# Fused chunk-sparse attention and ELU MLP on one core: a list scheduler with optional TensorE fillers, a lane model for DMAs, and another set of order parameters

## The chip, the core and the metric

The kernel runs on one core of one Trainium2 chip. The metric is device time in microseconds (us), lower is better. The kernel before takes 299.21 us, the median of three runs (298.0 to 299.57). TensorE is called PE here, its weight loads PEld, VectorE DVE, ScalarE ACT, GpSimd POOL and SyncE SP.

## The reference

Attention over 4 batches, 8 heads, 768 positions and 64 dimensions, in which each query keeps only 6 of 24 chunks of 32 keys, followed by an MLP with the ELU function. Cut to what matters:

```python
k_min = np.min(k_chunks, axis=3); k_max = np.max(k_chunks, axis=3)       # per chunk of 32 keys
ub = np.sum(np.maximum(q * k_min, q * k_max), axis=-1)                  # bound per query and chunk
ub = np.where(causal, ub, -1e9)
top_chunks = np.argsort(ub, axis=-1)[..., -6:]
scores = np.where(selected & causal_by_position, scale * q @ k.T, -1e9)
attn = softmax(scores)
x = (attn @ v) rearranged to [3072, 512]
h = x @ w_in                                                             # 512 -> 2048
out = where(h > 0, h, exp(min(h, 0)) - 1) @ w_out                        # 2048 -> 512
```

## The kernel before, in words

**Tiling.** The work is cut into eight parts i = 0 to 7: batch b = i // 2 and half h = i % 2 of the 768 positions, 384 queries each. Heads go in four pairs r = 0 to 3. For each part there are four kinds of work:

- `load` and `prep` (lines 415 to 515), once per pair: six DMAs of 96 KB bring K, Q and V of two heads (`kf`, `qf`, `vf`; line 412 issues them). TensorE transposes K and Q against an identity (L455), ACT or DVE copies them out of PSUM (L461, L463), DVE reduces K to chunk minima and maxima (L475), POOL or DVE places copies in `lhs` and `rhs` (L465), and POOL casts V to bf16 (L512). The casts are collected in the list `casts` in the order of the parts and pairs.
- `select` (lines 517 to 573), once per part, for all four pairs: TensorE forms the bounds (L529), DVE transposes them (L542), finds the sixth largest with MAX8 (L551), compares (L557), transposes back (L563) and writes the mask rows into `rhs` (L571).
- `attend` (lines 579 to 682), once per pair: scores (L595), exp on ACT into `pt` (L607, L613), the causal triangle on DVE (L622, L631), P·V (L651), the division on DVE (`rcp` L662, `on` L665), a transpose on TensorE (L676) and a copy to `xt` (L681). A pair of the second half uses five `pt` tiles, one of the first half two.
- `mlp` (lines 684 to 734), once per part: 16 groups of four matmuls with w_in (L693), for each of them exp on ACT (`e` L701), minus one on POOL (`m` L705) and ELU on DVE (`gT` L709); then three output tiles of 16 matmuls with w_out (L720) over all 16 `gT`, a copy (L728, L730) and a store.

The weights come in four pieces each, by casting DMAs on POOL's queue (`load_w_in` L365, `load_w_out` L372). Piece n waits for the V cast whose count stands in `T["gate"]`: the first four entries are for w_in, the last four for w_out, and an entry of 9 means the ninth cast.

**Fillers.** Lines 744 to 754 make operations called "fill": two matmuls of zeros, 512 columns wide, into a free PSUM bank (L750), with the lowest priority. Each one depends on the one before the last.

**What sets the order.** Nothing is emitted as it is written. `Graph.op` records each operation with its possible engines, costs, buffers, dependences and a priority, and `Graph.run` (lines 109 to 245) goes through time, event by event, and gives each idle engine the operation of lowest priority number that is ready and for which its buffers are free. The order in which operations start in this plan is the order in which they are emitted, on all engines, and each engine's instructions run in that order on the chip. `T` (lines 41 to 44) holds the number of buffers of each kind (`kf`, `pt`, `gT` and others) and the priorities: `attw` and `mlp` place the attention parts and the MLP parts, `prepa` and `loada` bring preparation and loads forward, `vlate` sets V loads and casts back, `sela` moves `select`, `evo`, `mf` and `sf` shift single steps, `gate` is for the weights, `fill` is the number of fillers.

In the plan, a DMA issued by SP or ACT may start while fewer than eight such transfers are under way (`flying[1] < 8`); which eight does not matter, and the count falls when the bytes are moved. The plan ends when every operation has been placed, the fillers too (`left`).

Of the kernel before, what the change touches and what calls it, by code (L numbers as in the profile page):

```python
# [36 lines left out]
PE, ACT, DVE, POOL, SP = "PE", "ACT", "DVE", "POOL", "SP"  # L37
SEM = 45.0


T = dict(kst=8, ubT=1, pstep=0.1397, kf=4, qf=4, vf=8, pt=9, xt=6, gT=18, qt=5, qr=4, rhs=5,
         nfirst=4, vlate=6.3955, gate=[2, 2, 6, 7, 7, 8, 9, 10], attw=[9.917, 18.912],
         mlp=[13.416, 15.5], loada=0.7909, prepa=10.9783, sela=-2.0944, fill=40, cold=6,
         evo=0.1849, mf=0.2655, sf=0.7044)


class Buf:
# [19 lines left out]
class Graph:  # L67
# [41 lines left out]
    def run(self, at=None, dma_lat=(700.0, 900.0)):  # L109
        free = {n: [(0.0, s) for s in range(len(v))] for n, v in self.slots.items()}  # L110
        engines = (PE, ACT, DVE, POOL, SP)
        at = {e: (at or {}).get(e, 0.0) for e in engines}
        avail = {e: [] for e in engines}
        events = sorted({0.0, *at.values()})
        arriving = []
        rings = {e: [] for e in (SP, ACT, POOL)}
        share = {SP: 1.0, ACT: 1.0, POOL: 7.0}
        flying = [0, 0]
        dma_at, asked = 0.0, -1.0
        port_free = {DVE: 0.0, POOL: 0.0}  # L120
        for o in self.ops:
            o.wait = len(o.deps)
            o.ready = 0.0
            if o.wait == 0:
                heapq.heappush(arriving, (0.0, o.seq, o))
        left = len(self.ops)
        order = []

        def settle(o):
            for b in o.bufs:  # L130
                b.left -= 1
                b.end = max(b.end, o.finish + SEM)
                if b.cls == "bank":
                    b.used[o.engine] = o.finish + SEM
                    heapq.heappush(events, o.finish + SEM)
                if b.left == 0 and b.cls in free:
                    free[b.cls].append((b.end, b.slot))
                    heapq.heappush(events, b.end)
            for n in o.nexts:
                n.wait -= 1  # L140
                n.ready = max(n.ready, o.finish + SEM)
                if n.wait == 0:
                    heapq.heappush(arriving, (n.ready, n.seq, n))
                    heapq.heappush(events, n.ready)

        def transfer(t):
            nonlocal dma_at, asked
            if asked <= t:
                asked = -1.0
            while True:  # L150
                live = [(r, share[e]) for e, r in rings.items() if r and r[0][0] <= dma_at]
                total = sum(w for _, w in live)
                later = [r[0][0] for r in rings.values() if r and r[0][0] > dma_at]
                stop = min([t] + later)
                if live:
                    stop = min(stop, dma_at + min(r[0][1] / w for r, w in live) * total)
                    for r, w in live:
                        r[0][1] -= (stop - dma_at) * w / total
                dma_at = stop
                for r, _ in live:  # L160
                    if r[0][1] <= 1e-6:
                        o = r.pop(0)[2]
                        flying[o.engine != POOL] -= 1
                        o.finish = dma_at + dma_lat[1]
                        settle(o)
                if dma_at >= t:
                    break
            live = [r for r in rings.values() if r]
            if live:
                due = max(t, min(r[0][0] for r in live)) + min(r[0][1] for r in live) + 1.0  # L170
                if not due - 40.0 < asked <= due + 40.0:
                    asked = due
                    heapq.heappush(events, due)

        while left or any(rings.values()):
            if not events:
                held = {n: len(v) for n, v in free.items()}
                stuck = [o.name for e in engines for _, _, o in avail[e]][:40]
                raise RuntimeError(f"stuck: {left} left, free {held}, {stuck}")
            t = heapq.heappop(events)  # L180
            while events and events[0] <= t:
                heapq.heappop(events)
            transfer(t)
            while arriving and arriving[0][0] <= t:
                _, _, o = heapq.heappop(arriving)
                for e in o.engines:
                    bisect.insort(avail[e], (o.prio, o.seq, o))
            moved = True
            while moved:
                moved = False  # L190
                for e in engines:
                    if at[e] > t:
                        continue
                    lst = avail[e]
                    pick = None
                    i = 0
                    while i < len(lst):
                        o = lst[i][2]
                        if o.start is not None:
                            lst.pop(i)  # L200
                            continue
                        ok = o.xfer is None or e == POOL or flying[1] < 8
                        need = {}
                        for b in o.bufs if ok else ():
                            if b.slot is None:
                                need[b.cls] = need.get(b.cls, 0) + 1
                                if sum(ft <= t for ft, _ in free[b.cls]) < need[b.cls]:
                                    ok = False
                                    break
                            elif b.cls == "bank" and any(x != e and ft > t for x, ft in b.used.items()):  # L210
                                ok = False
                                break
                        if ok:
                            pick = o
                            lst.pop(i)
                            break
                        i += 1
                    if pick is None:
                        continue
                    o = pick  # L220
                    dur, lat = o.engines[e]
                    o.engine, o.start = e, t
                    if e == POOL or (e == DVE and o.port):
                        held = max(0.0, port_free[DVE if e == POOL else POOL] - t)
                        dur, lat = dur + held, lat + held
                        port_free[e] = t + dur
                    at[e] = t + dur
                    heapq.heappush(events, at[e])
                    for b in o.bufs:
                        if b.slot is None:  # L230
                            fl = free[b.cls]
                            k = min((ft, s, j) for j, (ft, s) in enumerate(fl) if ft <= t)[2]
                            b.slot = fl.pop(k)[1]
                    if o.xfer is None:
                        o.finish = t + lat
                        settle(o)
                    else:
                        flying[e != POOL] += 1
                        rings[e].append([t + dur + dma_lat[0], o.xfer, o])
                        heapq.heappush(events, t + dur + dma_lat[0] + o.xfer)  # L240
                    order.append(o)
                    left -= 1
                    moved = True
        self.span = max(o.finish for o in order)
        return order
# [28 lines left out]
def kernel(  # L274
# [16 lines left out]
    def slots(cls, n, shape, dtype, pool=const):  # L291
        store[cls] = [pool.tile(shape, dtype, name=f"{cls}{i}") for i in range(n)]
        g.cls(cls, range(n))
# [4 lines left out]
    slots("bank", 8, [P, 512], F32, psum)  # L298
    slots("kf", T["kf"], [P, 3, 2, D], F32)
    slots("qf", T["qf"], [P, 3, 2, D], F32)  # L300
    slots("vf", T["vf"], [P, 3, 2, D], F32)
    slots("kt", 3, [P, HS], BF16)
    slots("lhs", 8, [P, 2, S], BF16)
    slots("vext", 8, [P, 6, 2, D + 1], BF16)
    for h in range(2):
        slots(f"rhs{h}", T["rhs"], [P, 2, HS], BF16)
    slots("kst", T["kst"], [P, 2, CHUNK], F32)
    slots("qt", T["qt"], [P, HS], F32)
    slots("qr", T["qr"], [P, HS], F32)
# [488 lines left out]
```

## Time and profile before

| | |
|---|---|
| median of 3 runs | 299.21 us (298.0 to 299.57) |
| the profiled execution's own time | 297.61 us |
| its span, first to last instruction | 295.8 us |
| mean granted clock of TensorE | 0.988 |
| PE busy (matmuls) | 282.7 us, 96% of the span |
| PEld busy (weight loads) | 173.0 us, 58% |
| DVE busy | 223.3 us, 75% |
| ACT busy | 202.0 us, 68% |
| POOL busy | 134.8 us, 46% |
| filler matmuls (L750) | 21.5 us of PE in 76 recorded matmuls |
| SP and ACT loads, POOL weight loads | 24.39 + 0.79 MB and 4.19 MB |

The span is also cut into 40 equal slices of 7.4 us, with the busy tenths of each engine, the clock that TensorE was granted and the share of the 16 DMA engines. A share over 1 means that packets overlapped on an engine. The busy time of a matmul reaches beyond the start of the next one, since matmuls are pipelined: 64 of the 384-column matmuls of L693, 329 ns each by their row, take 10.40 us one after another. A stretch of 5 us with PE at 5.00 is therefore full, and what is inside it is counted by starts. The chain of waits goes from the last instruction back to what released it, step by step; "issue" in it is time with no cause in the trace.

### The profile page before, as it was taken

To read this page: it belongs to the slowest core of one execution; us is meant where nothing else is said; L and a number is where in the kernel's file an instruction comes from. 1 tells how busy PE (TensorE), PEld (TensorE's weight loads), DVE (VectorE), ACT (ScalarE), POOL (GpSimd) and SP (SyncE) were. 2 spreads that over 40 slices of the span, in tenths; PEclk is the share of its full clock that TensorE was granted. 3 is DMA by queue.
4 is the path that set the end of the run, shared out by engine and by line. 5 is a ranking of instruction groups with operands and counts; after the bars stand their busy time and mean duration, and the time that the engine had idled before them with its cause. 6 is when DMAs were issued, how large, how long until landed. Compare 5 with 4: busy or idle time off the path is not lost.

```text
span 295.8 us, 7141 instructions
## 1 busy us (share of the span) xinstructions
PE 282.7 (96%) x2455; PEld 173.0 (58%) x2480; DVE 223.3 (75%) x650; ACT 202.0 (68%) x440; POOL 134.8 (46%) x292
## 2 busy tenths in 40 slices
PE   8799959989999999999999999999999999999995
PEld 4356626656666556765766467656665566655642
DVE  8799898767889686987899768869899855821830
ACT  2578368855997639896788478995787387763721
POOL 5583744744479204853377104851276003600720
PEclk9999978999999999999999999999999999999999
DMA  8999799897787730243331313331100010001002
GB/s 166 215 170 215 153 193 215 150 194 174 179 206 167 180 106 37 57 110 87 96 97 43 90 38 91 72 90 38 38 37 2 0 73 37 2 35 70 4 0 106
DMA packets 84515, 29.82 MB, mean 101 GB/s; under 512 B 77312, under 2 KB 81408, under 8 KB 84480
## 3 DMA queue, kind: packets, MB, share of 16 engines
q1 hardware_dynamic: 77056, 24.39, 34.5%
q0 software_dynamic: 4224, 4.19, 9.0%
q10 hardware_dynamic: 3200, 0.79, 1.4%
q8 instruction: 19, 0.31, 0.5%
q14 instruction: 16, 0.13, 0.2%
HBM read 27.26 MB, written 6.29 MB: 113 GB/s over the span
## 4 chain that ended last, share of the span: by engine, by line
PE 81%; DMA 6%; DVE 5%; ACT 4%; issue 2%; POOL 1%; ACTq 1%; POOLq 0%
PE bank L720 27%; PE bank L693 24%; PE bank L595 10%; PE bank L651 6%; PE bank L455 5%; PE bank L750 4%; PE bank L529 3%; DMA w_out_sb<-in_moe_w_out_dram 3%; DMA qf<-in_q_dram 2%; PE bank L676 2%; ACT pt L607 2%; DMA vf<-in_v_dram 1%; POOL m L705 1%; ACT rhs L461 1%; DVE gT L709 1%
## 5 line engine op out<-in xcount | busy, mean ns | idle before, releaser
L705 POOL TENSOR_SCALAR m<-e 128x384 f32<-128x384 f32 x128 | 65.7, 522 | 72.3 <-ACT e L701 62.2
L720 PE MATMUL bank<-w_out_sb,gT 128*128 128x512 bf16 x363 | 90.6, 379 | 2.5 <-DMA w_out_sb<-in_moe_w_out_dram 1.3
L693 PE MATMUL bank<-xt,w_in_sb 128*128 128x384 bf16 x512 | 92.8, 329 | 0.0
L607 ACT ACTIVATE pt<-bank 128x384 bf16<-128x384 f32 (+1 forms) x160 | 75.1, 557 | 22.7 <-PE bank L595 22.7
L709 DVE SCALAR_TENSOR_TENSOR gT<-bank,m 128x384 bf16<-128x384 f32 x128 | 67.7, 551 | 16.4 <-POOL m L705 14.1
L701 ACT ACTIVATE e<-bank 128x384 f32<-128x384 f32 x128 | 60.8, 496 | 17.8 <-PE bank L693 15.7
L693 PEld LDWEIGHTS <-w_in_sb 128*128 128x128 bf16 x512 | 49.1, 98 | 30.6 <-issue 1.7
L720 PEld LDWEIGHTS <-gT 128*128 128x128 bf16 x384 | 36.6, 97 | 36.1 <-issue 1.6
L595 PE MATMUL bank<-rhs,lhs 96*128 96x384 bf16 (+2 forms) x288 | 52.4, 297 | 0.0
L465 POOL COPY lhs<-kt 64x384 bf16<-64x384 bf16 x57 | 28.8, 506 | 30.7 <-ACT kt L461 27.8
L475 DVE TENSOR_REDUCE kst<-bank 128x12 f32<-128x384 f32 x64 | 33.6, 549 | 4.3 <-PE bank L455 2.1
L595 PEld LDWEIGHTS <-lhs 96*128 96x128 bf16 x288 | 25.6, 100 | 15.8 <-issue 2.0
L461 ACT ACTIVATE rhs<-qt 64x384 bf16<-64x384 f32 x47 | 24.5, 522 | 5.2 <-DMA vf<-in_v_dram 3.2
L651 PEld LDWEIGHTS <-pt 128*128 128x128 bf16 x672 | 24.5, 98 | 5.9 <-issue 1.5
L728 ACT ACTIVATE o<-bank 128x512 f32<-128x512 f32 x19 | 11.4, 597 | 23.3 <-PE bank L720 23.3
L512 POOL TENSOR_SCALAR vext<-vf 128x384 bf16<-128x384 f32 x32 | 16.6, 524 | 22.9 <-PE bank L651 13.7
L651 PE MATMUL bank<-vext,pt 128*128 128x65 bf16 x672 | 25.9, 194 | 0.0
L613 ACT ACTIVATE pt<-bank 128x512 bf16<-128x512 f32 x32 | 19.8, 619 | 5.6 <-PE bank L595 5.1
L750 PE MATMUL bank<-zeros 128*128 128x512 bf16 x76 | 21.5, 412 | 1.5 <-DVE warm L341 1.3
L622 DVE TENSOR_TENSOR pt<-pt,tri 128x512 bf16<-128x512 bf16 x32 | 14.2, 444 | 8.7 <-ACT pt L607 8.5
L665 DVE TENSOR_TENSOR on<-bank,rcp 128x384 bf16<-128x384 f32 x32 | 17.7, 553 | 0.6
L461 ACT ACTIVATE kt<-bank 128x384 bf16<-128x384 f32 x27 | 13.2, 488 | 6.9 <-PE bank L455 6.2
(52 smaller groups left out, 244.9 us busy)
## 6 DMA issues: line engine op xcount, KB each, us to landing
kf<-in_k_dram SPq DMA_DIRECT2D x64, 96.0 KB, 2.7
vf<-in_v_dram SPq DMA_DIRECT2D x64, 96.0 KB, 2.9
out_dram<-o SPq DMA_DIRECT2D x24, 256.0 KB, 2.1
qf<-in_q_dram SPq DMA_DIRECT2D x56, 96.0 KB, 2.6
w_in_sb<-in_moe_w_in_dram POOLq DMA_DIRECT2D x4, 512.0 KB, 8.2
w_out_sb<-in_moe_w_out_dram POOLq DMA_DIRECT2D x4, 512.0 KB, 10.0
qf<-in_q_dram ACTq DMA_DIRECT2D x8, 96.0 KB, 3.3
```

Of the source, the lines that this page charges most:

```text
L461: nc.scalar.activation(out=dst(), in_=src(), func=AF.Copy)
L465: nc.gpsimd.tensor_copy(out=dst(), in_=src())
L475: nc.vector.tensor_reduce(out=ap(kst)[:, w, cs], in_=ap(bank)[:, 0:HS].rearrange("p (c w) -> p c w", w=CHUNK), axis=AX.X, op=op)
L595: nc.tensor.matmul(ap(banks[hd])[:, o + pc:o + pc + wd], lhsT=ap(ls)[0:96, hd, P * kb:P * (kb + 1)], rhs=ap(rs)[0:96, hd, c0 - HS * h:c0 - ...
L607: lambda e, hd=hd, pt=pt, banks=banks, wtot=wtot: nc.scalar.activation(out=ap(pt)[:, hd, 0:wtot], in_=ap(banks[hd])[:, 0:wtot], func=AF.Ex ...
L651: nc.tensor.matmul(o3v()[:, hd, qi, :], lhsT=ap(pt)[:, hd, P * qi + off:P * qi + off + P], rhs=ap(vx[b, r])[:, kb, hd, :], start=(kb == 0) ...
L693: nc.tensor.matmul(ap(bank)[:, 0:HS], lhsT=w_in_sb[:, kk, P * fc:P * (fc + 1)], rhs=ap(xT[b, h, kk]), start=(kk == 0), stop=(kk == NKK - 1))
L701: lambda e, eb=eb, bank=bank: nc.scalar.activation(out=ap(eb), in_=ap(bank)[:, 0:HS], func=AF.Exp),
L705: lambda e, eb=eb, mb=mb: nc.gpsimd.tensor_scalar(out=ap(mb), in0=ap(eb), scalar1=-1.0, scalar2=1.0, op0=AOT.add, op1=AOT.mult),
L709: lambda e, gt=gt, bank=bank, mb=mb: nc.vector.scalar_tensor_tensor(out=ap(gt), in0=ap(bank)[:, 0:HS], scalar=0.0, in1=ap(mb), op0=AOT.max ...
L720: nc.tensor.matmul(ap(bank), lhsT=ap(gts[fc])[:, P * tt:P * (tt + 1)], rhs=w_out_sb[:, fc, :], start=(fc == 0), stop=(fc == NFC - 1))
L750: nc.tensor.matmul(ap(bank), lhsT=zeros[:, 0:P], rhs=zeros, start=True, stop=True)
```

## The change

Three edits in `Graph.run` and a new set of parameters. Fillers no longer count in `left`, so the plan ends when all other work is placed, and it uses of the fillers, now up to 80, those for which it finds TensorE idle. The count `flying` is replaced by the list `lanes` of all DMAs of SP and ACT in the order in which they are placed: a further one may be placed once the eighth before it has finished, with the semaphore's 45 ns. The new `T` changes buffers, priorities, gates and the number of fillers. `nfirst` has no effect beyond 4, as there are four pairs. No arithmetic changes. The core of the diff:

```diff
-T = dict(kst=8, ubT=1, pstep=0.1397, kf=4, qf=4, vf=8, pt=9, xt=6, gT=18, qt=5, qr=4, rhs=5,
-         nfirst=4, vlate=6.3955, gate=[2, 2, 6, 7, 7, 8, 9, 10], attw=[9.917, 18.912],
-         mlp=[13.416, 15.5], loada=0.7909, prepa=10.9783, sela=-2.0944, fill=40, cold=6,
-         evo=0.1849, mf=0.2655, sf=0.7044)
+T = dict(kst=8, ubT=1, pstep=0.147, kf=8, qf=4, vf=7, pt=6, xt=8, gT=16, qt=6, qr=8, rhs=7,
+         nfirst=10, vlate=7.4186, gate=[3, 4, 7, 8, 8, 8, 9, 11], attw=[9.864, 18.912],
+         mlp=[13.376, 15.503], loada=1.2965, prepa=11.7909, sela=-1.2635, fill=80, cold=6,
+         evo=0.4181, mf=0.2397, sf=0.6886)
...
-        left = len(self.ops)
+        left = sum(o.name != "fill" for o in self.ops)
         order = []
+        lanes = []
...
-                        flying[o.engine != POOL] -= 1
...
-                        ok = o.xfer is None or e == POOL or flying[1] < 8
+                        ok = (o.xfer is None or e == POOL or len(lanes) < 8
+                              or (lanes[-8].finish is not None and lanes[-8].finish + SEM <= t))
...
-                        flying[e != POOL] += 1
+                        if e != POOL:
+                            lanes.append(o)
...
-                    left -= 1
+                    left -= o.name != "fill"
```

More of the change, by code (lines that the diff above doesn't have):

```diff
@@ L117, in run @@
         share = {SP: 1.0, ACT: 1.0, POOL: 7.0}
-        flying = [0, 0]
         dma_at, asked = 0.0, -1.0
```

## The prediction

> **What bounds the kernel now.** I read the 40 slices first, then busy time by stretches cut where the slices change, then TensorE's waits, and last the chain of waits, because a chain names a cause and the slices say where a cause can matter.
>
> ```profile
> PE   8799959989999999999999999999999999999995
> DVE  8799898767889686987899768869899855821830
> PEclk9999978999999999999999999999999999999999
> DMA  8999799897787730243331313331100010001002
> ```
>
> TensorE has nothing left to give after about the ninth slice (a slice is 7.4 us). The dips, the loss of clock and the full DMA engines all lie in front. The stretches (columns: length, then busy us of PE, PEld, DVE, ACT, POOL, then granted clock, DMA share, GB/s) make that exact:
>
> ```profile
> 34.50:37.80 3.30, 3.27 (x57) 1.90 (x54) 2.15 (x8) 0.98 (x2) 3.29 (x6) 1.00 0.75 134
> 37.80:40.20 2.40, 0.00 (x0) 0.00 (x0) 2.40 (x24) 2.31 (x5) 1.83 (x4) 1.00 1.21 196
> 40.20:47.10 6.90, 5.92 (x23) 3.15 (x24) 6.75 (x16) 4.62 (x11) 0.99 (x3) 0.51 1.22 197
> 47.10:65.40 18.30, 16.91 (x157) 10.85 (x156) 12.72 (x27) 12.51 (x30) 10.88 (x20) 1.00 1.08 192
> 65.40:292.40 227.00, 225.73 (x1999) 138.81 (x2017) 168.77 (x495) 161.44 (x354) 97.19 (x203) 1.00 0.29 76
> ```
>
> From 65.4 to 292.4 PE is busy 225.73 of 227.00 us, and the list of waits has no entry for its matmuls in there. So the time is: when TensorE is fed for good (now 65.4), plus what work is left then, plus the tail of 3.4. Whatever the plan does can pay only by getting more real matmuls done before about 65 us, and can lose anywhere after it.
>
> The fillers (L750) are 21.47 us of PE, and all of them start before 34.7. Then they are used up. From 37.77 to 41.18 PE stands still, and the clock is granted at half from 40.2 to 47.1. Two more waits show in the chain (start, length, what):
>
> ```profile
> 6.60 3.43 DMA vf<-in_v_dram
> 10.05 3.22 DMA qf<-in_q_dram
> 13.31 0.55 PE bank L455 x3
> ...
> 55.69 7.90 DMA w_out_sb<-in_moe_w_out_dram
> 63.59 0.04 issue
> 63.63 1.02 PE bank L720 x4
> ```
>
> The second line is the issue of the last early q load on ScalarE. It starts only when a V load that SyncE issued at 6.60 has landed, though it reads and writes nothing of V. That fits the eight lanes of the diff, each handed on in the order of emission. ScalarE is held behind it:
>
> ```profile
> 10.05 0.38 ACTq L412 DMA_DIRECT2D qf<-in_q_dram  x1
> 10.47 0.52 ACT L461 ACTIVATE rhs<-qt 64x384 bf16<-64x384 f32 x1 [3.21 <-DMA vf<-in_v_dram]
> ```
>
> So 3.21 us of ScalarE go, the fourth pair's q transposes wait to 13.31, and select of the first half, which needs all four pairs, with them.
>
> **The change, part by part.** The sum is made against the profiled execution, 297.61 us (span 295.8 and 1.8 around it); the median of the runs shown, 299.21, is 1.6 above, and I carry the gain over to it.
>
> *More fillers.* The cap goes from 40 to 80 pairs, none compulsory. Where the plan sees TensorE idle after 34.7 it can now put a pair, so the hole before 41.18 can be filled and the half clock avoided. In the half-rate stretch PE works from 41.18 to 47.1, 5.9 us, on 2.95 us of full-rate work: gain 2.9. Bounds: 0 (the plan sees no hole where the chip has one) to 3.4 (half of the 6.9 us). I take 2.9, since the hole follows directly on the last filler. The 3.4 us of standing still give nothing by this: fillers replace it, and the VectorE chain through it (transpose, MAX8, compare, transpose, 36.4 to 42.0 with no gap) is as long as before. If `on` of the fourth pair, now queued behind the MAX8s, is put ahead of them, up to 3.4 come back; if it goes further back, as much is lost; I take 0.
>
> The row on the clock: half rate was granted after 2.4 us of idle PE, and it lasted 6.9 us. The Trainium skill (TensorE: Matmul & The Clock Gate, section "Why this matters for your kernels") asks only that there be no idle gap over about 3 us between matmul bursts, and its Part 1 gives a 3.4 us window for either step; by that the clock need not have fallen here, or would have been back in half the time, and this term would be between 0 and 1.7, the estimate from that page. The trace decides for the longer one. The same page, Part 4, says that transposes don't count as busy for the gate; if so, the transposes in the row 34.50:37.80 had already started the idle count, and fillers among transposes matter more than their time says. That speaks against counting on any plan that leaves transposes without fillers for some microseconds; no run here separates it.
>
> *Lanes in the plan.* A DMA of SP or ACT is placed only once the eighth before it in the emission order has landed, 45 ns added; until then ACT may pick other work. The 3.2 us stall of ScalarE at 7.26 can go. Bounds: 0 (the q load still comes as the lane allows) to 3.4 (all of it reaches select). What is late next is DVE: busy 4.8 of 5 us in each stretch from 15 to 35, and idle 1.65 and more between 10 and 15. It passes an earlier start on almost whole. But DMA runs at a share of 1.1 to 1.2 from 5 to 15, so V loads move back for what q gains. I take 2.0. The later stalls of SP (one V issue from 42.5 takes 4.70 us) come with a DMA share of 1.22, so I put them down to bandwidth and give them nothing.
>
> *Gates and priorities.* w_in0 and w_in1, now after the second V cast, come after the third and the fourth; w_in2, w_in3, w_out0 and w_out3 move back by one cast; w_out1 and w_out2 keep theirs. The `w_out2` issue at 55.69 stands in POOL's queue behind the `m` of the first MLP and the V cast at 55.24, and lands 7.90 us later under full DMA; PE waits 1.33 for it, from 62.3. If the first MLP starts 4.9 us earlier (2.9 + 2.0), the `m`s ahead on POOL do so too, and the issue with them; the landing follows if DMA gives it room, which it does only by taking K, Q and V of the third half later. Bounds: the whole wait goes (+1.3) to the whole advance is eaten there (-4.9). I take +0.7, half of the wait, since PE has 20 of 48 scores of the second half undone at 65 to put in front.
>
> *Buffers.* Two more rhs0 tiles are two more memsets of 218 ns (row L353) on DVE at 3 us: 0.4, hidden in the 1.65 idle at 11.47; without it 0.4 on the chain. More K buffers (4 to 8) let K loads go earlier. `pt` goes from 9 to 6: a second-half pair holds five, so exps of the next pair wait for the P·V of this one. Price of one such wait with nothing beside it: P·V 0.92 and one exp 0.56, 1.5 us, four pairs in 41 to 65 make 6. It is hidden under first-layer matmuls (L693, 64 in 10.40 us); I take 0. `gT` from 18 to 16 removes the head start of two groups at a seam; 0, as the seam's matmuls are 10 us long.
>
> *Late fillers.* A pair costs 0.43 us (12 filler matmuls in 2.59 us). Before 34.7 it replaced idle time. After 65 there is none: the 227 us have 1.3 idle by the row, in small gaps. A filler put into a gap of 0.1 or 0.2 pushes the rest back by the remainder. Bounds 0 to 17 (40 pairs of 0.43). I take 0.9, three pairs that each cover a gap of 0.1, since the spare ones are first used in the holes in front.
>
> Sum: 2.9 + 2.0 + 0.7 - 0.9 = 4.7. From 297.6 that is 292.9, from the median 294.5.
>
> **Rivals.**
> *Still better.* `on` moves ahead of MAX8 as well (3.4), the q load gains its full 3.4, and the w_out2 wait goes (1.3): 2.9 + 3.4 + 3.4 + 1.3 = 11.0 less 0.9, so 289. For it: DVE idles 1.1 us at 35.3 and the V cast for the fourth pair is long done. Against: DVE is full from 15 to 35 and DMA to 65. Chance 0.20 for the band 287 to 291.5.
> *Swallowed.* What is won by 47 us is lost at `w_out2`, whose gate is the same cast; then 4.9 goes into a longer wait at 58 to 63 and 0 to 1 us is left: 298 to 300. The same time results if the change doesn't do what it says: fillers fall elsewhere, PE still stands still beyond 2.4 us, and the clock falls again. For it: DMA share 1.0 to 1.2 through 65. Against: scores are there to fill in. Chance 0.13.
> *Slower.* Fillers land in the steady part. Place: between 65 and 290, wherever the plan sees PE short of a ready group for an instant. Price 0.43 each less the gap that it fills; at 0.3 net, they pass the other gains (5.6) from 19 late pairs on; if the front gains only half of that, 15 to 30 pairs make 301 to 305.5. For it: up to 40 pairs more, a pair also takes one of eight PSUM banks, and PE after 65 hides nothing. Against: all 40 were gone by 34.7, and the hole in front alone takes eight. Chance 0.23.
> *Forecast,* 291.5 to 297.7: 0.44.
>
> **Numbers.** 0.5%, 1.5 us here, is about what a measurement of this kernel can tell from no change. Faster by more: 0.44 + 0.20 = 0.64; within: 0.13; slower: 0.23. The range leaves out the best end below 289 (about 0.08) and the dear end above 301 (0.12): 289 to 301.
>
> **What would show it.** Right: granted clock 1.00 from 6 us on, with L750 matmuls between 35 and 41; the q load on ACT's queue issued before 8 us and select's first matmul before 17.2; PE without a gap from some point before 62. Wrong: L750 after 65 us in number; a second stretch of half clock; PE waiting for w_out over 1.3 us; ACT waiting on PE for `pt`. If more than ten fillers stand after 65, or the chain still shows a DMA landing of over 3 us after 50, the forecast fails.

## The result, and the profile after

| | before | after |
|---|---|---|
| median (20 runs each) | 298.36 us (296.69 to 300.77) | 296.58 us (295.22 to 299.4) |
| ratio, 95% interval | 1 | 0.9935 [0.9908, 0.9962] |
| span of the profiled execution | 295.8 us | 293.6 us |
| its granted clock | 0.988 | 1.00 |

The change makes the kernel 0.65% faster, about 1.9 us, where 4.7 were forecast. The direction holds and the median lies in the range of 289 to 301; the size is under half of the forecast. Ratios here and below leave out executions that took over 1.5% more than the fastest of the same kernel; medians are of all executions.

The slices of the kernel after, on the same scale as those of before (there is no row of the clock, which is full throughout this execution):

```profile
PE   8799999999999999999999999999999999999998
...
DMA  9979899898777772342522013111100011002002
```

The dips of PE in the sixth and the ninth slice are gone. The DMA engines are as full up to the ninth slice as before. At the right edge PE ends on 8 where it ended on 5: it now works to the very end, and the stretches say on what (columns as before: length, busy us of PE, PEld, DVE, ACT, POOL, then granted clock, DMA share, GB/s):

```profile
37.80:40.20 2.40, 2.40 (x15) 1.38 (x14) 2.40 (x22) 2.33 (x6) 1.59 (x3) 1.00 1.14 169
40.20:47.10 6.90, 5.90 (x35) 3.21 (x34) 6.26 (x12) 6.31 (x16) 4.00 (x8) 1.00 1.21 196
...
285.60:289.70 4.10, 4.10 (x20) 1.86 (x19) 0.00 (x0) 0.00 (x0) 0.00 (x0) 1.00 0.36 128
289.70:293.60 3.90, 3.00 (x14) 1.18 (x12) 0.00 (x0) 0.60 (x1) 0.00 (x0) 1.00 0.18 67
```

Where PE stood still for 2.40 us it now works for 2.40, and in the 6.90 us behind that the clock is 1.00 instead of 0.51. In the last 4 us DVE and POOL have nothing left to do, and PE still issues matmuls. The chain of waits names them (start, length, what; lines are one further on than before, so L751 are the fillers, L721 the second layer):

```profile
...
10.04 3.11 DMA qf<-in_q_dram
...
56.08 7.03 DMA w_out_sb<-in_moe_w_out_dram
...
63.15 1.02 PE bank L721 x4
...
285.79 0.43 PE bank L751 x2
286.22 0.86 PE bank L721 x4
287.09 0.43 PE bank L751 x2
...
288.38 0.43 PE bank L751 x2
...
289.68 3.02 PE bank L751 x14
```

Three things are to be seen. The late q load is issued at 10.04, the same instant as before. The second last weight piece lands at 63.11, half a microsecond earlier than before. And three pairs of fillers stand between the last groups of the second layer, in the path (3 x 0.43 = 1.3 us), with seven more behind the last of them: from the last real matmul to the end it is 293.6 - 289.68 = 3.9 us, where it was 295.8 - 292.30 = 3.5. Of the 53 filler pairs of this plan 43 stand before 39.8 us, none between 40 and 285, and 10 here.

What was gained in front is counted by weight loads, one for each matmul, in the groups up to 65 us. Before, then after (columns: operation, tiles, count, busy us and mean ns, idle before them):

```profile
L595 PEld LDWEIGHTS <-lhs 96*128 96x128 bf16 x52 | 5.1, 109 | 3.7 <-issue 1.4 <-DVE rhs L571 0.4
L455 PEld LDWEIGHTS bank<-ident_f,kf 128*128 128x128 f32 x33 | 4.3, 149 | 2.9 <-ACT qt L461 1.5 <-POOL econst L346 0.3 <-issue 0.2
...
L455 PEld LDWEIGHTS bank<-ident_f,qf 128*128 128x128 f32 x30 | 3.5, 144 | 2.2 <-DMA qf<-in_q_dram 1.2 <-DMA kf<-in_k_dram 0.3 <-issue 0.3
...
L720 PEld LDWEIGHTS <-gT 128*128 128x128 bf16 x12 | 1.2, 97 | 2.4 <-issue 1.6
```

```profile
L596 PEld LDWEIGHTS <-lhs 96*128 96x128 bf16 x60 | 5.4, 97 | 4.8 <-issue 2.1
L456 PEld LDWEIGHTS bank<-ident_f,kf 128*128 128x128 f32 x36 | 4.8, 147 | 3.8 <-ACT qt L462 1.7 <-POOL econst L347 0.3 <-issue 0.2
L456 PEld LDWEIGHTS bank<-ident_f,qf 128*128 128x128 f32 x36 | 4.4, 141 | 2.3 <-DMA qf<-in_q_dram 1.1 <-issue 0.3
...
L721 PEld LDWEIGHTS <-gT 128*128 128x128 bf16 x22 | 2.1, 97 | 1.9 <-issue 0.3
```

Ten more matmuls of the second layer (0.216 us each, by 0.86 for four in the chain), eight more scores (taken as 0.125 each; two of them stand in the chain with 0.22 or 0.33) and nine more transposes of K and Q (0.109 each, by 0.66 for six) make 2.2 + 1.0 + 1.0 = 4.1 us of real work done earlier. The account closes: 4.1 in front, less 1.3 of fillers in the path and 0.4 behind it, is 2.4, and the spans differ by 2.2.

So two questions stood open. Did the fillers and the clock bring those 4.1, as forecast, or something else? And what do the ten late pairs cost over many runs?

### The profile page after: what moved, and what is told of

Read it like the earlier page. It is cut to its first block, busy times and chain, and to the rows that moved or that the text cites. A ratio compares the mean times of both kernels' runs of the same rounds, so it can differ in the third digit from the quotient of the medians.

```text
span 293.6 us, 7213 instructions
## 1 busy us (share of the span) xinstructions
PE 287.4 (98%) x2506; PEld 174.5 (59%) x2506; DVE 221.2 (75%) x654; ACT 202.3 (69%) x442; POOL 134.7 (46%) x288
## 4 chain that ended last, share of the span: by engine, by line
PE 84%; DMA 6%; ACT 3%; DVE 3%; POOL 1%; issue 1%; ACTq 1%; POOLq 0%
PE bank L721 27%; PE bank L694 24%; PE bank L596 10%; PE bank L652 6%; PE bank L751 6%; PE bank L456 6%; PE bank L530 3%; DMA qf<-in_q_dram 2%; DMA w_out_sb<-in_moe_w_out_dram 2%; PE bank L677 2%; ACT pt L608 2%; POOL m L706 1%; DMA vf<-in_v_dram 1%; DVE gT L710 1%; DVE pt L632 1%
## 5 line engine op out<-in xcount | busy, mean ns | idle before, releaser
L721 PE MATMUL bank<-w_out_sb,gT 128*128 128x512 bf16 x384 | 94.4, 379 | 0.2 <-DMA w_out_sb<-in_moe_w_out_dram 0.2
L694 PE MATMUL bank<-xt,w_in_sb 128*128 128x384 bf16 x512 | 91.2, 326 | 0.0
L710 DVE SCALAR_TENSOR_TENSOR gT<-bank,m 128x384 bf16<-128x384 f32 x128 | 67.5, 553 | 13.5 <-POOL m L706 11.3
L721 PEld LDWEIGHTS <-gT 128*128 128x128 bf16 x384 | 36.1, 97 | 34.5 <-issue 0.6
L596 PE MATMUL bank<-rhs,lhs 96*128 96x384 bf16 (+2 forms) x288 | 51.5, 290 | 1.1 <-ACT pt L608 0.9
L466 POOL COPY lhs<-kt 64x384 bf16<-64x384 bf16 x57 | 30.0, 526 | 18.3 <-ACT kt L462 16.7
L751 PE MATMUL bank<-zeros 128*128 128x512 bf16 x106 | 28.6, 403 | 1.3 <-DVE warm L342 1.3
L462 ACT ACTIVATE rhs<-qt 64x384 bf16<-64x384 f32 x49 | 25.5, 521 | 5.8 <-DMA vf<-in_v_dram 3.2
L462 ACT ACTIVATE kt<-bank 128x384 bf16<-128x384 f32 x27 | 13.2, 491 | 8.1 <-PE bank L456 8.0
```

The lines of the kernel that those rows point to most:

```text
L462: nc.scalar.activation(out=dst(), in_=src(), func=AF.Copy)
L466: nc.gpsimd.tensor_copy(out=dst(), in_=src())
L596: nc.tensor.matmul(ap(banks[hd])[:, o + pc:o + pc + wd], lhsT=ap(ls)[0:96, hd, P * kb:P * (kb + 1)], rhs=ap(rs)[0:96, hd, c0 - HS * h:c0 - ...
L694: nc.tensor.matmul(ap(bank)[:, 0:HS], lhsT=w_in_sb[:, kk, P * fc:P * (fc + 1)], rhs=ap(xT[b, h, kk]), start=(kk == 0), stop=(kk == NKK - 1))
L710: lambda e, gt=gt, bank=bank, mb=mb: nc.vector.scalar_tensor_tensor(out=ap(gt), in0=ap(bank)[:, 0:HS], scalar=0.0, in1=ap(mb), op0=AOT.max ...
L721: nc.tensor.matmul(ap(bank), lhsT=ap(gts[fc])[:, P * tt:P * (tt + 1)], rhs=w_out_sb[:, fc, :], start=(fc == 0), stop=(fc == NFC - 1))
```

## The experiments

Each kernel's ratio is to the kernel before, run between its own runs on the same chip, over five rounds. No arithmetic changes in any of them: fillers multiply zeros, and the rest is order. The medians of before in the three sets were 298.98, 298.98 and 298.78 us.

### The late fillers left out

After `order = g.run(AT)` in the kernel after; plan times are ns, so only the ten pairs at the end go:

```diff
+    order = [o for o in order if o.name != "fill" or o.start < 1e5]
```

> The kernel after, with the ten filler pairs of the last 4 us left out (three pairs between the last four groups of the second layer, seven pairs behind the last one); everything else is emitted in the same order. Theory A (the late fillers stand in the path of TensorE and cost what they take): the three pairs are 1.29 us, the seven behind delay the end marker by up to 0.4, so the span falls from 293.6 to about 292.0, the time by 1.3 to 1.7 us, ratio to the kernel before about 0.988 to 0.990. Rival B (the end is set by the last copy and store, and TensorE would have waited in those places anyway): no change, ratio about 0.9935.

0.9863 [0.9827, 0.9898], median 295.36. Its chain of waits ends so:

```profile
280.22 10.37 PE bank L721 x48
290.62 0.60 ACT o L729
```

The second layer's last 48 matmuls run in one piece, and what ends the chain is again the copy out of PSUM. Against the change's own ratio this is 0.7%, some 2.2 us, and the two intervals do not meet; the trace had given 1.3 + 0.4. The loss at the end is therefore shown, by taking it away. In this profile the wait for the `w_out2` landing was 1.8 us, where the profile of after shows 0.2: that wait differs from run to run with the same front.

### The fillers in the hole left out, the late ones kept

```diff
+    order = [o for o in order if o.name != "fill" or not 30e3 < o.start < 1e5]
```

> The kernel after, without its fillers between about 31 and 40 us (nine pairs; the ones at the end stay). Theory A (fillers keep the clock, and that is the main gain of the change): TensorE idles some 3.9 us of 32 to 40, half clock is granted for one stretch of 6.8 us from about 40.2, granted clock near 0.988 on the mean, and the time rises by 2 to 3 us against the kernel after, ratio about 1.000 to 1.004. Rival B (the new order closed the hole, so the fillers are not needed): clock stays at 1.0, time as the kernel after or 0.4 less.

0.9894 [0.985, 0.9938]. The clock did not fall at 40 us in its profile (it fell once in the first 17 us), though PE idled 1.7 us ahead of the first MLP, and the kernel is no slower than the whole change (medians 296.71 here, 296.58 and 297.01 there). A loss of 2 to 3 us is not there. In the new order the first MLP starts sooner after the last select, so that PE stands still for 1.7 us without fillers and not for the 3.4 us of before.

### The fillers in the hole alone, in the old order

In the kernel before, in the loop that emits the plan:

```diff
+            if o.name == "px003":
+                for _ in range(14):
+                    nc.tensor.matmul(ap(o.bufs[1]), lhsT=zeros[:, 0:P], rhs=zeros, start=True, stop=True)
```

> The kernel before, with seven more filler pairs (14 matmuls, 3.0 us) put in front of the transpose L676 at 41.18, where TensorE stands idle from 37.77; nothing else moves. Theory A (the clock is worth 2.9 us, and most of it reaches the end): clock 1.0 throughout, the stretch from 41.2 on runs at full rate, span 293.0 to 294.3, ratio about 0.990 to 0.995. Rival B (the gain is eaten at the w_out piece that lands at 63.6, whose issue stands behind the first MLP's V cast): the wait in front of L720 grows from 1.3 to 3 to 4 us and the ratio is 0.998 to 1.000. Rival C (fillers delay the transpose): slower, at most 0.4 us.

0.9975 [0.9935, 1.0015]. First the stretch of the half clock, then PE's timeline (start, busy, line, tiles; in brackets the idle before it and what ended it), both of this kernel:

```profile
40.20:47.10 6.90, 5.41 (x33) 2.70 (x32) 6.75 (x16) 4.96 (x13) 0.98 (x3) 1.00 1.22 197
```

```profile
62.97 1.02 PE L720 MATMUL bank<-w_out_sb,gT 128*128 128x512 bf16 x4 [1.92 <-DMA w_out_sb<-in_moe_w_out_dram]
```

The clock is 1.00 in the stretch where it was 0.51, exactly as the prediction's largest term wants, and 33 matmuls run there instead of 23. Of the 2.9 us that this should bring, 0.7 ± 1.2 reach the end. Much of it is gone before the stretch is over: at the full clock PE waits for VectorE, which is busy 6.75 of the 6.90 us in both kernels. By PE's timelines the second part of the first MLP starts at 45.26 instead of 45.96, 0.7 us sooner, and the 1.1 us at half clock that before still has from there are 0.6 more: by this estimate PE is 1.3 us ahead when the stretch ends. First PE's waits for VectorE inside the stretch in this kernel (us in all, times, longest), then pieces of the chain of before (start, length, what), which stays on VectorE all through it:

```profile
PE bank L595 <- DVE kst L475: 0.7, 1, 0.7
...
PE bank L693 <- DVE xt L681: 0.3, 1, 0.3
```

```profile
41.13 0.89 DVE selT L563
...
43.77 0.56 DVE kst L475
...
47.70 0.55 DVE lhs L438
```

Then PE comes sooner to the first group that needs `w_out2` and waits for it 1.9 us instead of 1.33, and for the fourth piece another 0.6. Real work done by 65 us, all kinds counted at their own rate, rose only from 33.1 to 33.9 us.

### The late q load put ahead by hand

The lane model was to free ScalarE from the wait at 7 to 10 us. It did not: the load is issued at 10.04 again, and in each kernel of this study but the next one it is issued between 9.96 and 10.33. By the trace it waits until SP's V load of 6.59 has landed, and it stands on ACT behind a copy that the plan puts ahead of it; the plan's model does not bring it earlier. In ACT's timeline of the kernel after:

```profile
10.46 0.52 ACT L462 ACTIVATE rhs<-qt 64x384 bf16<-64x384 f32 x1 [3.23 <-DMA vf<-in_v_dram]
```

3.23 us of ACT behind a load of V that it does not read, against 3.21 before. To learn what the forecast 2.0 would have been worth had the stall gone, the load was moved by hand ahead of that copy in the kernel after:

```diff
+    q_last = [o for o in order if o.name == "ld003" and o.engine == ACT][-1]
+    order.remove(q_last)
+    order.insert(next(n for n, o in enumerate(order) if o.name == "qt000"), q_last)
```

> The kernel after, with one DMA moved: the last early q load is emitted on ScalarE ahead of the first copy of q^T, and so takes a lane that a K load frees, not the one of the V load of 6.59. Nothing else moves. Theory A (the 3.2 us that ScalarE stands at 6.7 to 10.0 delay select of the first half by about 2): the q load is issued at about 7, select's first matmul starts near 15 in place of 17.0, and 1.5 to 2.5 us reach the end, ratio about 0.985 to 0.988. Rival B (DMA bandwidth and the emission order of the front set what comes next, fillers included): select starts up to 2 us earlier, but at 40 and 63 us all stands as before, ratio about 0.9935.

0.9986 [0.9939, 1.0033], twelve executions from 296.2 to 306.0 us: none of the change's gain can be seen any more, which neither theory expected. ACT's wait is gone, PE does the fourth pair's q transposes earlier, and select's first matmul starts at 15.02 instead of 16.92, as the first theory had it. But then the chain shows what is late next:

```profile
15.94 2.29 SPq L413
18.28 3.92 DMA kf<-in_k_dram
```

A K load that used to be there in time is now issued at 15.94 by SP and lands at 22.2, PE waits 1.6 us for K, and the first MLP starts at 40.2 instead of 39.7. The q load's wait did hold select of the first half, but what is won there is lost at the K load; moved alone, it brings nothing.

### The change again, beside other kernels

> The kernel after, unchanged, so that the edits of this study have it beside them on the same chip. All theories: ratio to the kernel before 0.991 to 0.996, granted clock 1.0 or 0.994, and the third piece of w_out landing at 62.5 to 64.5 us.

0.9936 [0.9899, 0.9973], the first result again. The third piece of w_out, expected at 62.5 to 64.5, landed at 66.03 in its profile. The front ran differently this time:

```profile
43.20:46.30 3.10, 2.10 (x12) 0.87 (x10) 3.04 (x8) 2.94 (x8) 2.39 (x5) 1.00 1.22 195
46.30:49.70 3.40, 3.40 (x14) 1.71 (x12) 2.56 (x7) 2.79 (x7) 0.69 (x2) 0.50 1.22 196
```

PE idles 1.0 us behind exps of ACT between 43.2 and 46.3, and for the next 3.4 us the clock is granted at half. So the clock falls now and then in the changed kernel too. Over all the runs that the comparisons use, by the granted clock of the run (a half-rate stretch of 3.4 us takes 0.006 off the mean):

| granted clock | before: runs, median | after: runs, median |
|---|---|---|
| 1.00 | none | 16, 295.5 us |
| about 0.994 | 9, 297.7 us | 12, 297.4 us |
| about 0.988 | 39, 298.3 us | 2, 299.0 us |
| about 0.982 | 25, 299.9 us | none |

The kernel before has 2.2 half-rate stretches per run, the one after 0.5. In the kernel after a stretch more goes with 1.6 to 1.8 us, about the 1.7 that half a clock loses in 3.4 us; in the kernel before with 0.6 from the first to the second row and 1.6 to the third. This is a comparison of runs and not an experiment, but it agrees with the third experiment: in the old order not all that the clock loses reaches the end. And at one clock, 0.994, the two kernels are 0.3 us apart, with the 2.2 us of the late fillers in the kernel after.

### The issue of `w_out2` put ahead, in the old order

If the wait for `w_out2` swallows the gain, then moving its issue on POOL's queue, from behind the first MLP's `m`s to ahead of them, should set it free. Once with the hole fillers of the third experiment, once alone:

```diff
+    x = next(o for o in order if o.name == "w_out2")
+    order.remove(x)
+    order.insert(next(n for n, o in enumerate(order) if o.name == "m0.2"), x)
```

> The kernel before with the seven filler pairs in the hole (as in e3) and the issue of the third piece of w_out moved on POOL's queue from behind the V cast at 55.24 to in front of the third m of the first MLP (about 48 us); nothing else moves. Theory A (what the full clock wins is eaten at this landing, which holds at 63 us): landing near 57 to 59, no wait of L720 on it, and now the clock shows: span 292 to 293.5, ratio 0.985 to 0.990. Rival B (DMA is full at 48 us, so the piece lands no earlier than 62, or K, Q and V of the next parts come later by the same and TensorE waits for them): ratio 0.996 to 1.002.

> The kernel before with the third piece of w_out issued early (in front of the third m, about 48 us) and nothing else. Theory A: without the fillers TensorE reaches the place at 62.3 and waited 1.3 us, so 1.0 to 1.5 us are won and no more, ratio 0.995 to 0.997; the difference to e6 is then the price of the half clock, 2 to 3 us. Rival B: 0.999 to 1.004.

With the fillers 0.9973 [0.9938, 1.0008], alone 0.998 [0.9949, 1.001]: neither can be told from the third experiment (0.9975). The chain of the first of the two shows what came in the way:

```profile
59.64 7.78 DMA w_out_sb<-in_moe_w_out_dram
...
67.46 1.02 PE bank L720 x4
```

`w_out2` was issued at 49.6 and is no longer waited for. But now it is the fourth piece, issued at 59.64 behind the same `m`s and a V cast, that lands at 67.4, and PE waits 0.7 us for that. In the other kernel it lands at 68.0, and PE waits 1.9 us. One wait was moved and another took its place. The first profile also had the half clock once in front (14.0 to 17.6 us), with the first MLP at 43.07 instead of 41.20, so its wait is not the whole account.

### Both pieces put ahead, in the old order

The same edit with `w_out2` ahead of `m0.2` and `w_out3` ahead of `m0.6`, with the hole fillers:

```diff
+    for name, at in (("w_out2", "m0.2"), ("w_out3", "m0.6")):
...
```

> The kernel before with the seven filler pairs in the hole (as e3) and both late pieces of w_out issued early, the third in front of the third m, the fourth in front of the seventh m of the first MLP. In e6 only the third was early, and the wait went to the fourth, which landed at 67.5. Theory A (the pieces of w_out are what eats the clock's gain): no wait of L720 on w_out, span 291.5 to 293.5, ratio 0.983 to 0.990. Rival B (order of TensorE's other work and the loads that come later): ratio 0.994 to 1.000, with TensorE waiting on K, Q or V loads, or on VectorE, between 60 and 80 us.

0.9946 [0.9912, 0.9981], or 1.6 us, half of what was hoped for, and near the 1.3 that the stretch itself leaves by the estimate above; from the third experiment it can't be told apart. The profiled execution took 300.34 us, where the median is 296.98, so it shows which waits can come, not what they cost as a rule (tile, what it waits for: us in all, times, longest):

```profile
PE bank L720 <- DVE gT L709: 3.5, 1, 3.5
...
POOL vext L512 <- DMA vf<-in_v_dram: 5.8, 1, 5.8
```

No wait for w_out is left. In this execution what w_out gained, a V load lost: its cast stands on POOL's queue ahead of the `m`s, they wait with it, and PE waits for the `gT` behind them. The DMA engines have a share of 1.2 from 40 to 55 us in it, so one transfer put ahead made another late. Whether the usual executions lose anything in this way is not shown.

### The same on the change: late fillers out, `w_out2` ahead

```diff
+    order = [o for o in order if o.name != "fill" or o.start < 1e5]
+    x = next(o for o in order if o.name == "w_out2")
+    order.remove(x)
+    order.insert(next(n for n, o in enumerate(order) if o.name == "m0.7"), x)
```

> The kernel after without its ten late filler pairs (as e1) and with the third piece of w_out issued in front of the eighth m of the first MLP (about 49 us) in place of 56.1. Theory A (landing and late fillers are what is left): span 291 to 292, 0 to 1 us under e1, no wait over 0.2 for w_out in any run, so also a narrower spread than e1; ratio 0.982 to 0.986. Rival B (TensorE is full from 45 on in the order of the kernel after and has nothing to wait for; an earlier w_out only delays loads): as e1 or up to 1 us worse, ratio 0.986 to 0.990.

0.9853 [0.9814, 0.9892], median 293.52, and five of six runs within 293.39 to 293.82. By its median this is the fastest version, 0.8% under the change as made, which ran beside it (0.9936). No wait for w_out is in its profile. Against the first experiment (0.9863, six runs from 293.8 to 295.9, in another set) the medians can't be told apart; the move seems to take away the runs in which `w_out2` is late, but six runs do not show that.

### The change's code and its parameters, one without the other

Late fillers left out in both, to be set beside the first experiment. First the new code with the old `T` and `fill=80`; then the new `T` and the optional fillers, but with the old count of DMAs (this edit is shown against the kernel after):

```diff
...
-         mlp=[13.376, 15.503], loada=1.2965, prepa=11.7909, sela=-1.2635, fill=80, cold=6,
...
+         mlp=[13.416, 15.5], loada=0.7909, prepa=10.9783, sela=-2.0944, fill=80, cold=6,
```

> The two edits of the code (lanes, optional fillers up to 80) with the parameters T of the kernel before, late filler pairs left out so that they don't hide the order. To be set beside e1, which has the new T. Theory A (the lane model is what sets w_out2's groups later and puts other work in front of them; its plan has them 1.5 us later than the plan of before): ratio 0.986 to 0.991, near e1. Rival B (the new parameters bring the gain): ratio 0.994 to 1.000.

```diff
-                        ok = (o.xfer is None or e == POOL or len(lanes) < 8
-                              or (lanes[-8].finish is not None and lanes[-8].finish + SEM <= t))
+                        ok = o.xfer is None or e == POOL or flying[1] < 8
```

> The parameters T of the kernel after and optional fillers with the old count of transfers under way in place of the lanes, late filler pairs left out. Theory A (lanes bring the gain): ratio 0.994 to 1.000. Rival B (parameters bring it, the two DMA models place almost the same): ratio 0.984 to 0.990, as e1.

The code alone gives 0.993 [0.99, 0.9961], the parameters alone 0.9914 [0.9885, 0.9944]; both together gave 0.9863. Neither part holds the gain: 0.70% and 0.86% make 1.56%, against 1.37%. The fillers are in both parts and so counted twice; the excess of 0.2% is about what they brought alone in the third experiment (0.25%), though each of these figures has ±0.3 to 0.4% to it. Taken apart so, the lane model is worth 1.37 - 0.86 = 0.5%, 1.5 us, and the parameters 0.7%, 2.0 us, each with ±0.5%, so that the first is not clear of nothing. Neither kernel of this pair starts the first MLP earlier than before (43.05 and 41.80 against 41.48, fillers fill the time up to there), but in both profiles the clock was at half for 3.4 us once in front (from 13.2 and 13.4 us), which that of before did not have. In both ACT is held at 10 us as ever. What they do have is more real work by 65 us: 15 and 13 matmuls of the second layer against 12, 54 and 58 scores against 52, 66 and 69 transposes against 63, some 1.2 and 1.6 us by the prices above.

### No fillers in the hole, in the fastest version

```diff
+    order = [o for o in order if o.name != "fill" or o.start < 30e3]
...
```

> The kernel of e8 (after, no late fillers, third piece of w_out early) without its nine filler pairs between 31 and 40 us. e8 had five of six runs within 0.5 us and full clock, so this is the clean measure of what the fillers of the hole are worth in the new order. Theory A (they keep the clock): half clock for 3.4 or 6.8 us in most runs, 1.5 to 3 us over e8, ratio 0.990 to 0.996. Rival B (in the new order the idle time is cut up by transposes and stays under what the clock gate needs): clock 1.0, ratio 0.983 to 0.987, as e8.

0.9858 [0.9814, 0.9902], against 0.9853 with them in another set: no difference that these intervals of ±0.4% can show. The stretch with the hole, and PE's wait in it:

```profile
37.10:39.30 2.20, 0.67 (x5) 0.31 (x4) 2.20 (x26) 2.12 (x6) 2.14 (x4) 1.00 0.92 121
```

```profile
PE bank L694 <- DVE xt L682: 1.5, 1, 1.5
```

PE idles 1.5 us and the clock holds. In the two runs at full clock this kernel takes 292.6 and 292.7 us, less than any run with the fillers; at 0.998 one took 295.0, at 0.994 it takes 294.3 and 294.4, and one run at 0.987 took 296.3. In the profiles the fillers delay most of the first MLP by 0.6 us (39.90 against 39.32), and a fall of the clock goes with some 1.7 us. In this order they look like an insurance at its price; six runs do not show more.

## Why the prediction was right and wrong

**What bounds the kernel** held. Only work moved ahead of about 65 us counted, and after it any matmul more is paid in full. Direction and the closing account (4.1 - 1.3 - 0.4 = 2.4) come from that.

**The sum** failed on both sides by about as much. The front was put at 2.9 + 2.0 + 0.7 = 5.6 us; without the late fillers the change gives 1.37% or 4.1 us. The late fillers were put at 0.9; they cost 2.2. The two shortfalls, 1.5 and 1.3, are the whole of 4.7 against 1.9. That 4.1 comes near 5.6 is luck in good part: as the terms below show, little of it came by the ways that were summed, as far as the experiments reach.

**More fillers, 2.9 us.** The effect was read rightly: with fillers in the hole the clock is 1.00 in the same stretch. The step that failed is from the clock to the end of the kernel. "Gain 2.9" took a stretch of PE's own time as worth its length. But VectorE's chain does not end at 42.0, where the prediction stopped reading it: in the chain of before it goes on to 49.2, through the whole stretch at half clock, and with the clock restored PE waited 1.0 us for it inside the stretch. Behind that the DMA engines were at a share of 1.0 to 1.2 through 65 us, and the next matmuls stood behind weight pieces that these deliver (2.5 us of waiting instead of 1.33). Alone in the old order the term brought 0.7 ± 1.2; in the new one no worth of the fillers shows. This is the rival called swallowed, at work inside the forecast's largest term, though by the estimate of the third experiment (1.3 us ahead at the end of the stretch) more than half of it happened before `w_out2`.

**Lanes, 2.0 us.** The step named in the prediction, that "the 3.2 us stall of ScalarE at 7.26 can go", failed outright: 3.23 against 3.21. Freed by hand it starts select 1.9 us earlier, so the link to select was right, but it brings nothing at the end, as K is late next and not, as the prediction had it, DVE. If the lane model is still worth its 0.5 ± 0.5%, that comes by another way, since the stall is as long as before.

**Gates, 0.7 us.** The wait for `w_out2`, 1.33 before, is 0.2 in the profile of after, but 1.8 and 1.3 in two further ones with the same order in front. That is 0.2 us less on the mean, so 0.7 was too much as far as three profiles show. The moves of the issue showed that this wait alone is not worth much in the old order, as the fourth piece is late in its stead.

**`on` of the fourth pair, taken as 0.** It did go ahead of MAX8, and the first MLP starts at 39.66 instead of 41.48. The prediction gave the bound (up to 3.4) and took neither end. With the ten second-layer matmuls, the scores and the transposes that the new order has at hand before `w_out2` lands, this is the side on which the front won: order, which the prediction priced at nothing beyond w_out. How much of it is `on` alone was not tried.

**Late fillers, 0.9 us.** The rival's mechanism came, at a place that the prediction had not looked at: not in gaps of the steady part, where there are none, but in the last output tile, where the plan makes each group of matmuls wait for the one before and so sees PE idle between them. On the chip PE runs such groups without a gap (48 in 10.37 us). The seven behind them are there because the plan goes on until the last store's bytes are moved. The prediction counted three pairs in gaps of 0.1; there were ten, three of them in the path at their full 0.43 and seven behind it. Its own sign of failure, "more than ten fillers" after 65, was just missed if pairs are counted and met if matmuls are (ten pairs, twenty matmuls), and the other, a landing of over 3 us in the chain after 50, was met in full (7.03).

**The half-rate stretch.** The prediction set the row (half rate after 2.4 us of idle PE, for 6.9 us) against the Trainium skill, "TensorE: Matmul & The Clock Gate". That page, in "What's actually happening" of its Part 1, describes a free-running window of 3.41 us, after one of which, idle or busy, the clock changes. The half-rate stretches in the profiles here last 3.4 or 6.9 us, the length of one window or two, which agrees, so the 6.9 us of the row need no other rule. Its advice in "Why this matters for your kernels", no idle gap over about 3 us, is too generous for what was seen here: in the run of the change again a fall came after 1.0 us of idle, with PE busy 2.10 of 3.10 us.

**Left open.** Whether `pt` cut from 9 to 6 causes the wait for ACT at 43 to 46 us (1.0 us) was not separated. Nor was what decides, at equal idle time, whether the clock falls: from 42.9 to 46.3 us PE is busy 2.40 of 3.40 us both in the first profile of after, where the clock held, and in the second, where it fell; and in the kernel without fillers in the hole it held with 1.73 of 3.40 (35.9 to 39.3). And which part of the new order brings how much of the 4.1 us stays open, beyond the split into code and parameters.

## What to carry to other kernels

A faster stretch, be it a clock restored or a hole filled, is worth only what the next resource lets through: look up what the freed engine meets next, follow the chain of waits through the whole stretch, see how full the next supplier is, and price the step by that. A test of one part by itself in the old order says quickly whether a large visible loss reaches the end. Optional filler work needs a place where it stops: a planner that counts an in-order engine as idle between dependent instructions will put fillers into the last microseconds, where those between real matmuls are paid in full.

## What the runs showed of the hardware

- A half-rate stretch of TensorE's clock lasts 3.4 us or twice that in the profiles here, and it needs no long standstill: with PE busy 2.40 of the 3.40 us ahead the clock fell once and held once, and with 1.73 of 3.40 it held once.
- A DMA issued by ACT was held until another engine's unrelated load had landed, and ACT's queue with it, for 3.1 to 3.5 us in every profile but that of the moved load, with the old and the new model in the plan.
- With the DMA engines at a share of 1.2 the rows above show 195 to 197 GB/s, and 25 to 30 us of before 225 (share 1.18). A 512 KB piece of w_out took 7.9 to 13.5 us from issue to landing before and 7.0 to 15.4 after. Put ahead in the old order, one made the next piece late.
